# Attention over two K/V caches: batches taken in turn by head groups in the first 32 units

## The chip, the cores and the metric

The kernel runs on one core of a Trainium2 chip. The core has five engines that run their own instruction streams: TensorE (PE: matmuls, and transposes done as matmuls with an identity), VectorE (DVE), ScalarE (ACT), GpSimd (POOL) and SyncE (SP, which issues nearly all DMAs here). They meet through semaphores. The metric is the time of one execution in microseconds (us), as the median of several runs. One execution was also recorded by the profiler, and all durations below come from it.

## The reference

Two independent attention blocks, A and B, of the same shape, whose outputs are put side by side. Each has 16 batches, 144 query rows, 16 heads of 256, a cache of 512 keys, and a model width of 448:

```python
q = (x @ wq).reshape(B, Sq, H, Dh), heads ahead of rows
scores = einsum("bhqd,bhkd->bhqk", q, k_cache) * (Dh ** -0.5)
p = softmax(scores, axis=-1)
o = einsum("bhqk,bhkd->bhqd", p, v_cache)
out = o (rows ahead of heads, reshaped to B, Sq, H * Dh) @ wo
```

Everything is in bfloat16, with sums in float32.

## The kernel before

**Units.** A unit U is one head of one batch of one block: 512 units in all, 0 to 255 for A. `unit(U)` (line 228) says which; before the change heads run fastest, so units 0 to 15 are batch 0, units 16 to 31 are batch 1. Four units share one V load (`t_load_v`, group G), eight share one K load (`t_load_k`, group SG).

**Stages of one unit, by name.** Q: the projection `x @ wq` of this head, transposed, eight matmuls into a PSUM bank (line 398), copied to `qt_sb` by DVE or ACT (lines 411, 415). The 144 query rows are split into 112 (A rows) and 32 (B rows). SA: scores of the 112 rows (line 516); then a negated max on DVE (528), exp with row sums on ACT (539), a reciprocal on DVE (549), the normalisation on POOL (557). TA: four transposes of the probabilities (570), copied by DVE (580). SB: the scores of the 32 rows of eight units at once into two banks, sb0 and sb1 (440); their max, exp, norm, transpose TB (493) and copy (502) are done for four units together. PV: probabilities by V (603), copied by ACT into `ring` (618). OP: the output projection of 128 finished rows, a chunk, in 32 pieces, one matmul each (641).

**Order.** No engine reorders. A loop over slots i (lines 779 to 864) writes out the streams: in slot i it emits the loads that are due, Q of the units with `q_slot` i, SB of the group with `sb_slot` i, SA of unit i+5, TA of unit i+2, PV of unit i, K transposes with `kt_slot` i, and output projection pieces. `_Sched.add` puts in a wait for each true dependence, for each reused buffer and for each PSUM bank that another engine used last. In the steady pattern the stages of a unit U are emitted from slot U-15 (Q) to slot U (PV); for the first 24 Q, the first two SB and the first 16 K transposes the slots are written by hand (lines 686 to 689).

**Loads.** `plan(lo, deadline, lead, ...)` gives each load a deadline and an earliest slot. All are sorted by deadline and emitted in that order, so SP's queue is one row of loads; a load whose buffer is still in use holds up those behind it. Three K groups, three V groups and three x groups have room in SBUF.

**The start.** K of the first 16 units is loaded as it lies (`t_load_k_nat`, four loads of 1 MiB, kn0 to kn3) and transposed on PE (`t_kt`: eight transposes into a bank, one copy of 128 x 1024 by DVE or ACT, line 359). From group 2 on, K is transposed by the DMA itself (`t_load_k`, 2 MiB, line 368). The x rows of the first four batches are loaded as they lie too and transposed on PE (`t_xt`, line 329). These natural tiles lie in the space of `wo_sb` and of K slot 2, so wo of block A (eight loads of 448 KB) can come only when they have been read. A few matmuls that nobody reads (`t_warm`) stand around the x transposes. Q alternates between the banks qp and op up to unit 15 and has only qp after that, as op serves the output projection.

Of the kernel before, what the change touches and what calls it, by code (L numbers as in the profile page):

```python
# [122 lines left out]
def bass_concat_heads__mha_block_cached__gqa_block_cached__near_ridge_kernel(  # L123
# [54 lines left out]
    with contextlib.ExitStack() as es:  # L178
# [33 lines left out]
        kt_nat = (kt0_nat, kt1_nat)  # L212
        sem_names = list(COMPUTE) + ["ostt0", "ostt1", "xn", "kn0", "kn1", "kn2", "kn3"]
        for i in range(NK):
# [13 lines left out]
        def unit(U):  # L228
            pr, r = divmod(U, NU)
            b, h = divmod(r, H)  # L230
            return pr, b, h
# [45 lines left out]
        def t_load_wo(pr, wg):  # L277
            c0 = wg * WOG
            w = wos[pr]

            def e(q):
                return q.dma_start(wo_sb[:, c0:c0 + WOG, :],
                                   w[c0 * 128:(c0 + WOG) * 128, :].rearrange("(c p) n -> p c n", p=128)).then_inc(
                    sems["wo%d" % wg], 16)
            x = [(("kn", 2), 1), (("kn", 3), 1), (("xn", 0), 1)] if pr == 0 else []
            S.add(SP, e, writes=[(("wo", wg), pr)] + x, dma_sem="wo%d" % wg, name="wo%d.%d" % (pr, wg))

        def t_load_x(XG):
            pr, j = divmod(XG, Bn // XB)
            sl = XG % NXG  # L290
            x = xs[pr][j * XB:(j + 1) * XB].rearrange("b q d -> (b q) d")

            def e(q):
                q.dma_start_transpose(xt_sb[:, sl, 0:3, :], x[:, 0:384]).then_inc(sems["xt%d" % sl], 16)
                return q.dma_start_transpose(xt_sb[:, sl, 3, :], x[:, 320:448]).then_inc(sems["xt%d" % sl], 16)
            S.add(SP, e, writes=[(("xt", sl), XG)], dma_sem="xt%d" % sl, n_dma=2, name="x%d" % XG)

        def t_load_x_nat():
            x = xs[0][0:XB].rearrange("b q d -> (b q) d")
            nf = XB * SQ // 128  # L300

            def e(q):
                q.dma_start(x_nat[:, 0:nf, :], x[0:nf * 128, :].rearrange("(t p) d -> p t d", p=128)).then_inc(
                    sems["xn"], 16)
                return q.dma_start(x_nat[0:XB * SQ - nf * 128, nf, :], x[nf * 128:XB * SQ, :]).then_inc(sems["xn"], 16)
            S.add(SP, e, writes=[(("xn", 0), 0)], dma_sem="xn", n_dma=2, name="xn")

# [9 lines left out]
        def t_xt(k):  # L317
            key, bank, acc = ((("sbb", 0), "sb0", ptb_ps[0]), (("sbb", 1), "sb1", ptb_ps[1]),
                              (("sap", 0), "sa0", pta_ps[0]))[k]
            n = (256, 256, XB * SQ - 512)[k]  # L320
            dst = acc[:, 0:4 * n].rearrange("p (c r) -> p c r", c=4)

            def e(t):
                ins = None
                for r0 in range(0, n, 128):
                    m = min(128, n - r0)
                    for kc in range(4):
                        c0 = min(128 * kc, D - 128)
                        ins = t.transpose(dst[:, kc, r0:r0 + m], x_nat[0:m, 2 * k + r0 // 128, c0:c0 + 128],
                                          ident[0:m, 0:m])  # L330
                return ins
            S.add(PE, e, reads=[(("xn", 0), 0), ("ident", 0)], writes=[(key, ("x", k))], banks=[bank], name="XT%d" % k)

            def ev(v):
                o = xt_sb[:, 0, :, 256 * k:256 * k + n]
                return v.activation(o, dst, AF.Copy) if k == 1 else v.tensor_copy(o, dst)
            S.add(ACT if k == 1 else DVE, ev, reads=[(key, ("x", k))], writes=[(("xt", 0), 0)], banks=[bank],
                  name="ext%d" % k)

        def t_kt(u):  # L340
            ot = ((("otp", u % 2), "ot%d" % (u % 2), ot_ps[u % 2].bitcast(BF16)))
            key, bank, acc = ot if u < 12 else ((("sbb", 0), "sb0", ptb_ps[0]) if u % 2 else
                                                ("opp", "op", op_ps.bitcast(BF16)))

            def e(t):
                ins = None
                for c in range(KR):
# [5 lines left out]
                  name="KT%d" % u)  # L353
            eng = ACT if u % 2 else DVE

            def ev(v):
                o = kt_sb[:, u // 8].rearrange("p k d r -> p (k d) r")[:, :, (u % 8) * 128:(u % 8 + 1) * 128]
                src = acc[:, 0:1024].rearrange("p (j r) -> p j r", j=8)
                return v.activation(o, src, AF.Copy) if eng == ACT else v.tensor_copy(o, src)
            S.add(eng, ev, reads=[(key, ("k", u))], writes=[(("kt", u // 8), u // 8)], banks=[bank], name="ekt%d" % u)  # L360

        def t_load_k(SG):
            pr, r0 = divmod(8 * SG, NU)
            sl = SG % NK
            src = ks[pr].rearrange("b h k d -> (b h k) d")[r0 * SK:(r0 + 8) * SK, :]

            def e(q):
                return q.dma_start_transpose(kt_sb[:, sl].rearrange("p k d r -> p (k d) r"),
                                             src.rearrange("(r k) d -> r (k d)", k=KR)).then_inc(sems["kt%d" % sl], 16)
# [12 lines left out]
        def q_bank(U):  # L382
            return (op_ps, "opp", "op") if U < 16 and U % 2 else (qp_ps, "qp", "qp")

        def t_q(U):
# [7 lines left out]
            def e(t):  # L393
                ins = None
                for kc in range(4):
# [26 lines left out]
        def t_warm(k):  # L422
            def e(t):
                ins = None
                for _ in range(N_WARM[k]):
# [3 lines left out]
                  name="W%d" % k)  # L429

        def t_sb(SG):
            ksl = SG % NK

            def e(t):
                ins = None
                for dc in range(2):
# [71 lines left out]
        def t_sa(U):  # L508
            SG = U // 8
            ksl = SG % NK  # L510
            bank = U % 2

            def e(t):
                ins = None
                for dc in range(2):
                    ins = t.matmul(sa_ps[bank][0:QA, :].rearrange("q (k r) -> q k r", k=KR),  # L516
                                   lhsT=qt_sb[:, U % NQT, dc, 0:QA],
                                   rhs=kt_of(U, dc), start=(dc == 0), stop=(dc == 1))
                return ins
            S.add(PE, e, reads=[(("qt", U % NQT), U), (("kt", ksl), SG)], writes=[(("sap", bank), ("s", U))],  # L520
                  banks=["sa%d" % bank], name="SA%d" % U)
# [258 lines left out]
        while True:  # L780
# [141 lines left out]
```

## Time and profile before

| what | value |
|---|---|
| runs | 1203.04, 1200.89, 1197.51 us; median 1200.89 |
| profiled execution | 1198.11 us, span of the instructions 1196.4 us |
| busy share of PE, DVE, ACT, POOL | 99%, 65%, 63%, 57% |
| granted PE clock | 1.0 of full speed throughout |
| HBM read and written | 153.61 MB and 4.13 MB, 132 GB/s over the span |

A slot without output projection pieces lasts some 1.8 us, eight slots with them 18.0 us. PE is busy all through but for the first 55 us and the tail. The profile's tables give, for each engine, the busy time and the idle time ahead of groups of instructions with what ended it (the releaser); the timelines give start and duration of each.

### The profile page before, as it was taken

The numbers are of one execution on the slowest core, as the hardware profiler recorded it, in microseconds if no ns is written. First come the engines' busy times: TensorE is split into PE (matmuls) and PEld (weight loads), VectorE is DVE, ScalarE is ACT, GpSimd is POOL, SyncE is SP. The second block draws the span as 40 slices with busy tenths as digits, with TensorE's granted clock in tenths as the row PEclk, the third lists the DMA queues.
The fourth block names the chain that finished last, engine by engine and source line by source line (L and its number), as shares of the span: only waits on it lengthen the run. The fifth ranks groups of instructions, "written<-read, shape, count | busy, mean of one in ns | idle before, by whom it ended". The sixth has DMA issues, their size and how long they took to land.

```text
span 1196.4 us, 34155 instructions
## 1 busy us (share of the span) xinstructions
PE 1181.5 (99%) x14116; PEld 901.0 (75%) x14116; DVE 773.6 (65%) x2190; ACT 758.7 (63%) x2222; POOL 677.0 (57%) x680
## 2 busy tenths in 40 slices
PE   7899999999999999999999999999999999999998
PEld 5677777777777777777777777777777777777775
DVE  4666666666666666666666766666666666666664
ACT  4666666666666666666666666666666666666564
POOL 1565665655655655655655655656556656656554
PEclk9999999999999999999999999999999999999999
DMA  9999999999999999999999999999999999999971
GB/s 301 292 271 270 258 246 245 224 245 243 256 237 223 245 251 253 226 249 226 281 291 286 281 275 279 246 245 237 235 262 232 237 234 257 247 236 234 233 197 48
DMA packets 611130, 294.09 MB, mean 246 GB/s; under 512 B 529696, under 2 KB 538720, under 8 KB 610976
## 3 DMA queue, kind: packets, MB, share of 16 engines
q1 hardware_dynamic: 609344, 288.01, 102.3%
q0 software_dynamic: 1632, 3.90, 1.1%
q8 instruction: 112, 1.84, 0.6%
q14 instruction: 42, 0.34, 0.1%
HBM read 153.61 MB, written 4.13 MB: 132 GB/s over the span
## 4 chain that ended last, share of the span: by engine, by line
PE 94%; DVE 3%; SPq 1%; DMA 1%; ACT 0%; issue 0%; DVEq 0%
PE ot_ps L603 20%; PE qp_ps L398 20%; PE sa_ps L516 19%; PE op_ps L641 18%; PE sa_ps L570 8%; PE sb_ps L440 5%; PE sb_ps L493 2%; DVE stat L528 1%; DMA wq_sb<-in_A_wq_dram 1%; DVE pt_sb L580 1%; DVE stat L453 0%; PE qp_ps L641 0%; SPq L272 0%; SPq L274 0%; DVE qt_sb L411 0%; SPq L379 0%
## 5 line engine op out<-in xcount | busy, mean ns | idle before, releaser
L557 POOL TENSOR_TENSOR pa_sb<-pa_sb,stat 112x512 bf16<-112x512 bf16 x512 | 532.6, 1040 | 509.2 <-DVE stat L549 483.3
L539 ACT ACTIVATE pa_sb<-sa_ps,stat 112x512 bf16<-112x512 f32 x512 | 352.0, 688 | 404.9 <-DVE stat L528 404.0
L528 DVE TENSOR_REDUCE stat<-sa_ps 112x1 f32<-112x512 f32 x512 | 353.7, 691 | 324.6 <-PE sa_ps L516 323.9
L398 PEld LDWEIGHTS qp_ps<-xt_sb,wq_sb 128*128 128x128 bf16 x4032 | 283.3, 98 | 80.3 <-DMA wq_sb<-in_A_wq_dram 2.6
L603 PE MATMUL ot_ps<-pt_sb,v_sb 128*128 128x144 bf16 x4096 | 340.4, 226 | 0.0
L398 PE MATMUL qp_ps<-xt_sb,wq_sb 128*128 128x144 bf16 x4032 | 334.5, 226 | 5.9 <-DMA wq_sb<-in_A_wq_dram 3.3
L516 PE MATMUL sa_ps<-kt_sb,qt_sb 128*112 128x512 bf16 x1024 | 310.7, 385 | 1.4 <-DVE pt_sb L580 0.4
L641 PE MATMUL op_ps<-wo_sb,ring 128*128 128x448 bf16 x1120 | 278.8, 352 | 0.0
L603 PEld LDWEIGHTS ot_ps<-pt_sb,v_sb 128*128 128x128 bf16 x4096 | 268.5, 97 | 0.4
L570 PEld LDWEIGHTS sa_ps<-ident,pa_sb 112*128 112x128 bf16 x2048 | 145.6, 97 | 110.7 <-ACT pa_sb L539 26.2
L618 ACT ACTIVATE ring<-ot_ps 128x288 bf16<-128x288 f32 (+8 forms) x512 | 190.3, 372 | 4.4 <-PE ot_ps L603 4.4
L580 DVE COPY pt_sb<-sa_ps 128x448 bf16<-128x448 bf16 x512 | 190.4, 372 | 2.4 <-PE sa_ps L570 2.4
L570 PE MATMUL sa_ps<-ident,pa_sb 112*128 112x112 bf16 x2048 | 185.4, 212 | 0.2
L411 DVE TENSOR_SCALAR qt_sb<-qp_ps 128x288 bf16<-128x288 f32 x250 | 113.9, 455 | 71.8 <-PE qp_ps L398 71.3
L481 POOL TENSOR_TENSOR pb_sb<-pb_sb,stat 128x512 bf16<-128x512 bf16 x128 | 133.1, 1040 | 0.1
L516 PEld LDWEIGHTS sa_ps<-kt_sb,qt_sb 128*112 128x112 bf16 x1024 | 97.0, 129 | 39.4 <-issue 27.2
L641 PEld LDWEIGHTS op_ps<-wo_sb,ring 128*128 128x128 bf16 x1120 | 95.1, 98 | 27.6 <-ACT ring L618 0.2
L415 ACT ACTIVATE qt_sb<-qp_ps 128x288 bf16<-128x288 f32 x254 | 105.1, 414 | 14.3 <-PE qp_ps L398 10.1
L539 ACT ACTIVATION_READ_ACCUMULATOR pa_sb<-sa_ps,stat 112x1 f32 x512 | 99.0, 193 | 0.0
L463 ACT ACTIVATE pb_sb<-sb_ps,stat 128x512 bf16<-128x512 f32 x128 | 88.5, 692 | 0.0
L453 DVE TENSOR_REDUCE stat<-sb_ps 128x1 f32<-128x512 f32 x128 | 87.0, 680 | 0.0
L549 DVE RECIPROCAL stat<-stat 112x1 f32<-112x1 f32 x512 | 78.4, 153 | 0.7 <-ACT pa_sb L539 0.7
(49 smaller groups left out, 418.9 us busy)
## 6 DMA issues: line engine op xcount, KB each, us to landing
v_sb<-in_A_v_cache_dram SPq DMA_DIRECT2D x64, 1024.0 KB, 6.1
v_sb<-in_B_v_cache_dram SPq DMA_DIRECT2D x64, 1024.0 KB, 6.0
out_dram<-ost_sb POOLq DMA_DIRECT2D x34, 112.0 KB, 5.8
wo_sb<-in_A_wo_dram SPq DMA_DIRECT2D x8, 448.0 KB, 7.5
wo_sb<-in_B_wo_dram SPq DMA_DIRECT2D x8, 448.0 KB, 6.6
wq_sb<-in_A_wq_dram SPq DMA_DIRECT2D x4, 768.0 KB, 11.8
wq_sb<-in_B_wq_dram SPq DMA_DIRECT2D x4, 768.0 KB, 7.8
kt_sb<-in_A_k_cache_dram SPq DMA_DIRECT2D x2, 1024.0 KB, 11.0
```

Of the source, the lines that this page charges most:

```text
L398: ins = t.matmul(acc[:, dc * SQ:(dc + 1) * SQ], lhsT=wq_sb[:, kc, c0:c0 + 128], rhs=xt_sb[:, xsl, kc, xo:xo + SQ], start=(kc == 0 and dc = ...
L411: return v.tensor_scalar(qt_sb[:, sl, :, :], src, 1.0 / 16.0, None, op0=ALU.mult)
L481: return g.tensor_tensor(pb_sb[:, psl, :], pb_sb[:, psl, :], stat[:, RINVB + sl:RINVB + sl + 1].to_broadcast([128, SK]), op=ALU.mult)
L516: ins = t.matmul(sa_ps[bank][0:QA, :].rearrange("q (k r) -> q k r", k=KR), lhsT=qt_sb[:, U % NQT, dc, 0:QA], rhs=kt_of(U, dc), start=(dc = ...
L528: return v.tensor_reduce(stat[0:QA, NEG + sl:NEG + sl + 1], sa_ps[bank][0:QA, :], axis=AX.X, op=ALU.max, negate=True)
L539: return a.activation(pa_sb[0:QA, psl, :], sa_ps[bank][0:QA, :], AF.Exp, bias=stat[0:QA, NEG + sl:NEG + sl + 1], scale=1.0, accum_out=stat ...
L557: return g.tensor_tensor(pa_sb[0:QA, psl, :], pa_sb[0:QA, psl, :], stat[0:QA, RINV + sl:RINV + sl + 1].to_broadcast([QA, SK]), op=ALU.mult)
L570: ins = t.transpose(pta_ps[bank][:, c * 128:c * 128 + QA], src[:, c, :], ident[0:QA, 0:QA])
L580: return v.tensor_copy(pt_sb[:, sl, :, 0:QA], pta_ps[bank][:, 0:512].rearrange("p (c q) -> p c q", c=4)[:, :, 0:QA])
L603: ins = t.matmul(ot_ps[ob][:, dc * SQ:(dc + 1) * SQ], lhsT=v_sb[:, vsl, j, c * DH + dc * 128:c * DH + (dc + 1) * 128], rhs=pt_sb[:, sl, c, ...
L618: ins = a.activation(ring[:, 2 * h:2 * h + 2, c0:c0 + n1], src[:, :, 0:n1], AF.Copy)
L641: ins = t.matmul(acc[0:m, 0:D], lhsT=ring[:, c, col0:col0 + m], rhs=wo_sb[:, c, :], start=(c == first), stop=(c == last))
```

## The change

- **Order of units.** Units 0 to 15 are heads 0-3 of batch 0, heads 0-3 of batch 1, heads 4-7 of batch 0, heads 4-7 of batch 1. Units 16 to 23 are heads 8-15 of batch 0, units 24 to 31 those of batch 1. From unit 32 on nothing differs.
- **x.** The natural x load is split: 384 rows first, the other 192 late; the third group of transposes covers 192 rows, goes into bank op in slot 10, and only batches 2 and 3 wait for its copy (a resource of its own, xt2).
- **K transposes.** KT0 to KT4 are put behind Q3 to Q7; KT5 to KT7 end slot -7; KT8 to KT15 come one or two per slot in slots -2 to 3. Their banks and copying engines differ; each unit's K^T is a resource of its own (ktn), so SA of a unit waits for that unit's.
- **Q.** All of the first eight in slot -7, then one per slot behind SA, then two per slot in slots 4 to 7; two banks up to unit 23.
- **SB1** in slot 4 instead of 3.
- **Loads.** The order before was xn, wq0, kn0, wq1, kn1, wq2, kn2, v0, wq3, kn3, v1, v2, k2, wo 0-3, v3, v4, k3, v5, wo 4-7, v6, k4, v7, v8, k5. It becomes xn0, wq0, kn0, kn1, wq1, v0, kn2, kn3, v1, v2, wq2, wq3, xn1, k2, v3, v4, k3, v5, wo 0-3, v6, k4, v7, wo 4-7, v8, k5.

```diff
         def unit(U):
             pr, r = divmod(U, NU)
-            b, h = divmod(r, H)
+            if U < 16:
+                b, h = U // 4 % 2, U // 8 * 4 + U % 4
+            elif U < 32:
+                b, h = (U - 16) // 8, U % 8 + 8
+            else:
+                b, h = divmod(r, H)
...
+        def t_load_x_nat(k):
...
+                if k == 0:
+                    return q.dma_start(x_nat[:, 0:3, :], x[0:384, :].rearrange("(t p) d -> p t d", p=128)).then_inc(
+                        sem, 16)
+                q.dma_start(x_nat[:, 3, :], x[384:512, :]).then_inc(sem, 16)
+                return q.dma_start(x_nat[0:XB * SQ - 512, 4, :], x[512:XB * SQ, :]).then_inc(sem, 16)
...
         def t_xt(k):
             key, bank, acc = ((("sbb", 0), "sb0", ptb_ps[0]), (("sbb", 1), "sb1", ptb_ps[1]),
-                              (("sap", 0), "sa0", pta_ps[0]))[k]
-            n = (256, 256, XB * SQ - 512)[k]
+                              ("opp", "op", op_ps.bitcast(BF16)))[k]
+            c0, n = ((0, 256), (256, 128), (384, XB * SQ - 384))[k]
...
         def t_kt(u):
-            ot = ((("otp", u % 2), "ot%d" % (u % 2), ot_ps[u % 2].bitcast(BF16)))
-            key, bank, acc = ot if u < 12 else ((("sbb", 0), "sb0", ptb_ps[0]) if u % 2 else
-                                                ("opp", "op", op_ps.bitcast(BF16)))
+            if u < 4 or u in (6, 7):
+                key, bank, acc = ("otp", u % 2), "ot%d" % (u % 2), ot_ps[u % 2].bitcast(BF16)
+            elif u < 8:
+                key, bank, acc = ("sap", u % 2), "sa%d" % (u % 2), pta_ps[u % 2]
+            else:
+                key, bank, acc = ("sbb", int(u in (11, 13, 15))), "sb%d" % (u in (11, 13, 15)), ptb_ps[u in (11, 13, 15)]
...
-            eng = ACT if u % 2 else DVE
+            eng = ACT if u in (4, 6, 9, 11, 13, 15) else DVE
...
-            S.add(eng, ev, reads=[(key, ("k", u))], writes=[(("kt", u // 8), u // 8)], banks=[bank], name="ekt%d" % u)
+            S.add(eng, ev, reads=[(key, ("k", u))], writes=[(("ktn", u), 0)], banks=[bank], name="ekt%d" % u)
...
-            return (op_ps, "opp", "op") if U < 16 and U % 2 else (qp_ps, "qp", "qp")
+            return (op_ps, "opp", "op") if U < 24 and U % 2 else (qp_ps, "qp", "qp")
...
+        def kt_keys(us):
+            if us[0] < NKT:
+                return [(("ktn", u), 0) for u in us]
+            return [(("kt", us[0] // 8 % NK), us[0] // 8)]
...
-            S.add(PE, e, reads=[(("qt", U % NQT), U), (("kt", ksl), SG)], writes=[(("sap", bank), ("s", U))],
+            S.add(PE, e, reads=[(("qt", U % NQT), U)] + kt_keys([U]), writes=[(("sap", bank), ("s", U))],
...
-        sb_slot[0:2] = [-LS, 3]
+        sb_slot[0:2] = [-LS, 4]
         q_slot = [u - LQ for u in range(NT)]
-        q_slot[0:24] = [-7] * 4 + [-6] * 4 + [-5, -5, -4, -4, -1, -1, 0, 0] + [3, 4, 4, 5, 6, 6, 7, 8]
-        kt_slot = [-7] * 4 + [-6] * 4 + [-3, -3, -2, -2, 1, 1, 2, 2]
+        q_slot[0:24] = [-7] * 8 + [-5, -4, -3, -2, -1, 0, 1, 2] + [4, 4, 5, 5, 6, 6, 7, 7]
+        kt_slot = [-7] * 8 + [-2, -1, 0, 1, 2, 2, 3, 3]
...
-                dl = pr * NU + 4 * hg - LQ if pr > 0 else (-59, -57, -55, -52)[hg]
+                dl = pr * NU + 4 * hg - LQ if pr > 0 else (-59, -56, -49, -48)[hg]
...
-        plan(s_min, -60, 0, t_load_x_nat)
+        plan(s_min, -60, 0, t_load_x_nat, 0)
+        plan(s_min, -47, 0, t_load_x_nat, 1)
         for hf in range(4):
-            plan(s_min, (-58, -56, -54, -51)[hf], 0, t_load_k_nat, hf)
+            plan(s_min, (-58, -57, -54, -53)[hf], 0, t_load_k_nat, hf)
         for wg in range(NWG):
-            plan(3, 4 if wg < 4 else 9.5, 10 ** 6, t_load_wo, 0, wg)
+            plan(11, 9 if wg < 4 else 9.8, 10 ** 6, t_load_wo, 0, wg)
         for SG in range(2, NSG):
-            dl = {2: 2, 3: 8.5}.get(SG, 8 * SG - LSB)
+            dl = {2: 2, 3: 7, 4: 9.4}.get(SG, 8 * SG - LSB)
...
-            dl = (-53, -50, -49, 5, 6, 9)[G] if G < 6 else 4 * G
+            dl = (-55, -52, -51, 5, 6, 8, 9.2, 9.6)[G] if G < 8 else 4 * G
...
             if i == q_slot[0]:
                 t_warm(0)
-                for k in range(3):
+                for k in range(2):
                     t_xt(k)
                 t_warm(1)
-            for u in q_at.get(i, ()):
+            qs = q_at.get(i, ())
+            for u in qs if not -LS <= i < 4 else ():
                 t_q(u)
                 t_evac_q(u)
+                if i == q_slot[0] and u >= 3:
+                    t_kt(u - 3)
             for n in sbs.get(i, ()):
                 t_sb(n)
             u = i + LS
...
                 t_exp(u)
+            for u in qs if -LS <= i < 4 else ():
+                t_q(u)
+                t_evac_q(u)
...
             for u in kt_at.get(i, ()):
-                t_kt(u)
+                if u >= 5:
+                    t_kt(u)
+            if i == 10:
+                t_xt(2)
```

More of the change, by code (lines that the diff above doesn't have):

```diff
@@ L212, in bass_concat_heads__mha_block_cached__gqa_block_cached__near_ridge_kernel @@
         kt_nat = (kt0_nat, kt1_nat)
-        sem_names = list(COMPUTE) + ["ostt0", "ostt1", "xn", "kn0", "kn1", "kn2", "kn3"]
+        sem_names = list(COMPUTE) + ["ostt0", "ostt1", "xn0", "xn1", "kn0", "kn1", "kn2", "kn3"]
         for i in range(NK):
@@ L284, in e @@
                     sems["wo%d" % wg], 16)
-            x = [(("kn", 2), 1), (("kn", 3), 1), (("xn", 0), 1)] if pr == 0 else []
+            x = [(("kn", 2), 1), (("kn", 3), 1), (("xn", 0), 1), (("xn", 1), 1)] if pr == 0 else []
             S.add(SP, e, writes=[(("wo", wg), pr)] + x, dma_sem="wo%d" % wg, name="wo%d.%d" % (pr, wg))
@@ L295, in e @@
                 return q.dma_start_transpose(xt_sb[:, sl, 3, :], x[:, 320:448]).then_inc(sems["xt%d" % sl], 16)
-            S.add(SP, e, writes=[(("xt", sl), XG)], dma_sem="xt%d" % sl, n_dma=2, name="x%d" % XG)
-        def t_load_x_nat():
+            S.add(SP, e, writes=[(("xt", sl), XG)] + ([(("xt2", 0), 1)] if XG == NXG else []), dma_sem="xt%d" % sl, n_dma=2, name="x%d" % XG)
+        def t_load_x_nat(k):
             x = xs[0][0:XB].rearrange("b q d -> (b q) d")
-            nf = XB * SQ // 128
+            sem = sems["xn%d" % k]
             def e(q):
[L303 to L306, printed above, removed]
+                if k == 0:
[3 more added lines that the diff above has]
+                return q.dma_start(x_nat[0:XB * SQ - 512, 4, :], x[512:XB * SQ, :]).then_inc(sem, 16)
+            S.add(SP, e, writes=[(("xn", k), 0)], dma_sem="xn%d" % k, n_dma=1 + k, name="xn%d" % k)
         def t_load_k_nat(hf):
@@ L327, in e @@
                     for kc in range(4):
-                        c0 = min(128 * kc, D - 128)
-                        ins = t.transpose(dst[:, kc, r0:r0 + m], x_nat[0:m, 2 * k + r0 // 128, c0:c0 + 128],
+                        d0 = min(128 * kc, D - 128)
+                        ins = t.transpose(dst[:, kc, r0:r0 + m], x_nat[0:m, (c0 + r0) // 128, d0:d0 + 128],
                                           ident[0:m, 0:m])
                 return ins
-            S.add(PE, e, reads=[(("xn", 0), 0), ("ident", 0)], writes=[(key, ("x", k))], banks=[bank], name="XT%d" % k)
+            S.add(PE, e, reads=[(("xn", k // 2), 0), ("ident", 0)], writes=[(key, ("x", k))], banks=[bank], name="XT%d" % k)
             def ev(v):
-                o = xt_sb[:, 0, :, 256 * k:256 * k + n]
+                o = xt_sb[:, 0, :, c0:c0 + n]
                 return v.activation(o, dst, AF.Copy) if k == 1 else v.tensor_copy(o, dst)
-            S.add(ACT if k == 1 else DVE, ev, reads=[(key, ("x", k))], writes=[(("xt", 0), 0)], banks=[bank],
+            S.add(ACT if k == 1 else DVE, ev, reads=[(key, ("x", k))], writes=[(("xt2" if k == 2 else "xt", 0), 0)], banks=[bank],
                   name="ext%d" % k)
         def t_kt(u):
-            ot = ((("otp", u % 2), "ot%d" % (u % 2), ot_ps[u % 2].bitcast(BF16)))
-            key, bank, acc = ot if u < 12 else ((("sbb", 0), "sb0", ptb_ps[0]) if u % 2 else
-                                                ("opp", "op", op_ps.bitcast(BF16)))
+            if u < 4 or u in (6, 7):
[4 more added lines that the diff above has]
+                key, bank, acc = ("sbb", int(u in (11, 13, 15))), "sb%d" % (u in (11, 13, 15)), ptb_ps[u in (11, 13, 15)]
             def e(t):
@@ L359, in ev @@
                 return v.activation(o, src, AF.Copy) if eng == ACT else v.tensor_copy(o, src)
-            S.add(eng, ev, reads=[(key, ("k", u))], writes=[(("kt", u // 8), u // 8)], banks=[bank], name="ekt%d" % u)
+            S.add(eng, ev, reads=[(key, ("k", u))], writes=[(("ktn", u), 0)], banks=[bank], name="ekt%d" % u)
         def t_load_k(SG):
-            pr, r0 = divmod(8 * SG, NU)
+            pr, b, h = unit(8 * SG)
+            r0 = b * H + h
             sl = SG % NK
@@ L370, in t_load_k @@
             w = [(("kn", 0), 1), (("kn", 1), 1)] if SG == 2 else []
+            if 3 <= SG < 5:
+                w = [(("ktn", 8 * (SG - 3) + j), 1) for j in range(8)]
             S.add(SP, e, writes=[(("kt", sl), SG)] + w, dma_sem="kt%d" % sl, name="k%d" % SG)
@@ L401, in e @@
                 return ins
-            S.add(PE, e, reads=[(("wq", hg), pr), ("wqz", 0), (("xt", xsl), XG)],
+            S.add(PE, e, reads=[(("wq", hg), pr), ("wqz", 0), (("xt", xsl), XG)]
+                  + ([(("xt2", 0), 0)] if XG == 0 and b > 1 else []),
                   writes=[(key, ("q", U))], banks=[bank], name="Q%d" % U)
@@ L444, in e @@
                 return ins
-            S.add(PE, e, reads=[(("qt", (8 * SG + jj) % NQT), 8 * SG + jj) for jj in range(8)] + [(("kt", ksl), SG)],
+            S.add(PE, e, reads=[(("qt", (8 * SG + jj) % NQT), 8 * SG + jj) for jj in range(8)]
+                  + kt_keys(range(8 * SG, 8 * SG + 8)),
                   writes=[(("sbb", 0), ("s", 2 * SG)), (("sbb", 1), ("s", 2 * SG + 1))], banks=["sb0", "sb1"],
```

## The prediction

> **What bounds the kernel now.** I read the busy table first, then what TensorE (PE) waited for, then PE's timeline over the first 60 us, and last SP's queue and the DMA stretches that follow them.
>
> ```profile
> PE 1181.5 (99%) x14116; PEld 901.0 (75%) x14116; DVE 773.6 (65%) x2190; ACT 758.7 (63%) x2222; POOL 677.0 (57%) x680
> PE qp_ps L398 <- DMA wq_sb<-in_A_wq_dram: 3.3, 4, 1.3
> PE qp_ps L398 <- ACT qt_sb L415: 1.7, 1, 1.7
> PE qp_ps L398 <- DVE qt_sb L411: 0.9, 1, 0.9
> PE ot_ps L349 <- DMA kt_sb<-in_A_k_cache_dram: 0.9, 2, 0.6
> PE sb_ps L440 <- ACT kt_sb L359: 0.7, 1, 0.7
> ```
>
> PE is busy 1181.5 of 1196.4 us, so at most 14.9 us can be won without taking work off PE, and the waits listed (us, times, longest) all belong to the start: Q projections that wait for wq or for their one bank, transposes of K that wait for K, SB1 that waits for its last K^T copy. The change touches nothing but this start. The timeline has the places (start, duration, and idle before it in brackets):
>
> ```profile
> 31.36 0.67 PE L398 MATMUL qp_ps<-xt_sb,wq_sb 128*128 128x144 bf16 x8 [0.94 <-DMA wq_sb<-in_A_wq_dram]
> ...
> 50.83 0.67 PE L398 MATMUL qp_ps<-xt_sb,wq_sb 128*128 128x144 bf16 x8 [1.67 <-ACT qt_sb L415]
> ...
> 60.34 1.05 PE L440 MATMUL sb_ps<-kt_sb,qt_sb 128*32 128x512 bf16 x16
> ```
>
> The first is Q12, waiting for the fourth quarter of wq; the second is Q21, waiting for the copy that empties the only Q bank; the third is SB2. After 50.83 PE has no wait of that size until the tail. The other half of the picture is SP's queue (start, time that the issue held SP) and DMA stretches of 2 us, whose last two columns are DMA share and GB/s:
>
> ```profile
> 26.01 20.41 SPq L368 DMA_TRANSPOSE kt_sb<-in_A_k_cache_dram  x1
> ...
> 54.94 12.22 SPq L368 DMA_TRANSPOSE kt_sb<-in_A_k_cache_dram  x1
> 67.20 0.58 SPq L379 DMA_DIRECT2D v_sb<-in_A_v_cache_dram  x1
> 67.83 3.37 SPq L282 DMA_DIRECT2D wo_sb<-in_A_wo_dram  x4
> 71.24 2.28 SPq L379 DMA_DIRECT2D v_sb<-in_A_v_cache_dram  x1
> 73.56 14.63 SPq L368 DMA_TRANSPOSE kt_sb<-in_A_k_cache_dram  x1
> 88.24 1.14 SPq L379 DMA_DIRECT2D v_sb<-in_A_v_cache_dram  x2
> 89.42 13.86 SPq L368 DMA_TRANSPOSE kt_sb<-in_A_k_cache_dram  x1
> ```
> ```profile
> 84.00:86.00 2.00, 2.00 (x28) 1.61 (x26) 1.93 (x5) 1.37 (x5) 1.95 (x2) 1.00 1.20 87
> 86.00:88.00 2.00, 2.00 (x29) 1.73 (x27) 1.65 (x7) 1.62 (x5) 1.08 (x2) 1.00 1.28 290
> 94.00:96.00 2.00, 2.00 (x23) 1.43 (x22) 1.48 (x4) 1.07 (x5) 1.03 (x2) 1.00 1.05 395
> ```
>
> From 2 us to about 110 us the DMA engines are never long without work. The four K groups after the two naturally loaded ones (k2 to k5, 2 MiB each) land, by issue plus time to landing, at 26.0+23.1=49.1, 54.9+14.3=69.2, 73.6+16.7=90.3 and 89.4+18.1=107.5; their readers SB2 to SB5 start at 60.3, 78.4, 96.4 and 114.5. The margins are 11, 9, 6 and 7 us. What PE gains at the start is taken from these.
>
> **The sum, part by part.** I walked PE, DVE, ACT and POOL in program order, each instruction starting when its engine, its data and its bank are free. Distances come from the timelines: PE start to start Q 0.50, SA 0.43, SB 0.98, TA 0.20, PV 0.50, eight K transposes 0.44; to release 0.66 to 0.70 for Q, SA, PV and K^T; DVE max 0.61, K^T copy 0.60, Q copy 0.36; ACT exp with its accumulator read 0.68, K^T copy 0.90, Q copy 0.29; POOL 0.99. Done on the kernel before with its own landings, the walk puts SB0 at 22.85, PV0 at 35.0 and SB2 at 60.25, where the timeline has 22.97, 35.00 and 60.34: good to some 0.1 us there.
>
> *Load order.* The old landings (wq0 9.4, kn0 12.1, wq1 15.6, kn1 18.6, wq2 21.8, kn2 24.3, v0 27.6, wq3 31.3, kn3 33.8, v1 36.4, v2 39.1) give 2.5 to 3.3 us per MiB of K or V and 3.2 to 3.7 per wq quarter. In the new order, 0.16 MB of x stands behind, so wq0 is some 0.5 us earlier: wq0 8.9, kn0 11.6, kn1 14.6, wq1 17.9, v0 20.9, kn2 23.6, kn3 26.3, v1 29.0, v2 31.7, wq2 35.2, wq3 38.6, x's rest 39.1. k2 has the same bytes ahead and lands at 49.1 again.
>
> *Slot -7.* Q0 starts at 8.95 (before 9.46). Q0 to Q3, then Q4 to Q7 alternate with K^T, whose copies now end under the next Q: KT0 11.65, KT7 16.7, no idle between. Up to KT7 the old walk has 5.4 us of gaps, the new one 1.9. SB0 waits 1.0 for the copies of units 6 and 7 and starts at 18.1.
>
> *Slots -5 to 3.* One Q per slot, put behind SA; wq1 and kn2 have landed. Four waits stay or come, all behind softmax: SA2 on exp 0.4, SA3 0.7, SA5 0.4, and KT8, which now shares bank sb0 with TB0 and waits 1.0 for that copy. Behind KT8 on PE stand SA4 and all that follow, so this one counts in full.
>
> *Slots 4 to 10.* Q16 to Q23 take two banks in turn: the 0.9 and 1.7 us at Q18 and Q21 go, 0.2 stays at Q20. wq2 (35.2) is ahead of Q16 (37.0), wq3 (38.6) of Q20 (42.9). SB1 waits 0.4 for K^T 15, before 0.7 to 0.9. SA waits for its own unit alone, which lets SA8 pass ahead of SB1 and adds nothing to the sum.
>
> *The moved x part.* PE still makes 20 transposes of x; eight come at slot 10 with one DVE copy of 0.6 to 0.7. Their first reader is a Q of batch 2 seven slots on. Cost nothing; without that cover up to 0.7.
>
> SB2 comes out at 53.5 against 60.25: **6.7 us** less idle (6.9 against 13.6). If the K or V loads come 1 to 3 us later than I place them, the walk gives 5.5; if wq0 and K come 1 us sooner, 7.2.
>
> *Output projection.* Batch 0 ends at unit 23, not 15, so the first chunk starts at slot 25 instead of 17, and slots 17 to 24 are 1.8 us long instead of 2.25. At SB5 PE has done 32 pieces, before 46; the 14 missing ones (0.19 each, 2.6 us) come later at the same price. Idle saved by SB5, without any new wait, is 6.6 us, and SB5 would start at 105.2: 104.7 by the walk, plus the 0.5 by which it is early at SB5 of the kernel before.
>
> *wo moved on SP's queue.* wo 0 to 3 goes from behind k2 to behind v5, and wo 4 to 7 from behind v5 to behind v7. Behind the first stand v6 and k4, behind the second v8 and k5. Up to k5 the same bytes pass the same engines as before, and after k2 no PE wait holds SP up: PV7, which frees v4's buffer and with it k3, ends at 47.5, one microsecond after k2's issue ends. So from 49.1: v3 and v4 5.3 us, k3 8.4 to 10.8 (landing differences of k3, k4, k5 to the V before them), lands at 64.5 (SB3 69.0). The old stretch k3 to k4, with v, four wo, v and k in it, took 21.1 us; the new stretches to k4 and to k5 both have that content: k4 at 85.6 (SB4 87.3), k5 at 106.7. By SP's old issue times in the new order instead (k3 issued at 48.1, k4 at 66.6, k5 at 87.3 and 18.1 to landing), k5 lands at 105.4; with the slowest K, 10.8 us, three times, at 110. So SB5 waits 0 to 5 us, not less than nothing, since a load that lands early moves no start. I take 1.5, from the stretch that has the same content. k6 then lands 15 us after k5 at about 122, SB6 is at 125: no second wait.
>
> **Sum:** 6.6 - 1.5 = 5.1 us. The profiled execution took 1198.11 us (span 1196.4, 1.7 around it) and would take 1193.0. The median of the three runs is 1200.89, 2.8 above it: **1195.8 us**.
>
> **Rivals.**
>
> *No wait at SB5* (1194.3): k5 lands before 105.2, and the whole 6.6 us stays. For it: SP's issue times give 105.4. Against: the byte order gives 106.7. The Trainium skill ("Advanced Engine Details and Errata", section X-Bar Transpose (TRN2)) says that transposing DMAs run as fast as plain ones, 350 to 400 GB/s; by that each 2 MiB would take some 5.6 us as an estimate, k5 would land about ten microseconds sooner, and the time would be this rival's. The trace disagrees: 290 GB/s in the stretches of K against 395 in those of V, with slumps to 87.
>
> *More K waits* (1198 to 1200): SB4, with 1.7 us of margin, waits too, or v7 (89.4 against PV28 at 90.5), and k6 or k7 are late as well; each takes 1 to 2 us from the gain. For it: all these margins are under 3 us. Against: from 124 to 126 us the DMA share of the kernel before is down to 0.31, so there the queue catches up.
>
> *Slower* (1206): the K loads are held up so that the start's gain is spent twice. With 20 us from issue to landing (k2 took 23.1, k3 to k5 14.3 to 18.1), SP's chain is k3 68.1, k4 72.4+20=92.4, k5 96.5+20=116.5: SB5 waits 11.3 and 6.6-11.3 = -4.7. It costs more than the gain from 18.4 us on. Against: k2 had four loads in flight ahead of it, these have two or three.
>
> *That it does not do what it says:* SB0 needs all eight K^T of its group, so waiting for each alone may change nothing. The walk takes no time from it, and the forecast stands.
>
> **How the numbers follow.** Forecast 0.45 (its own range 1194 to 1198.5), no wait 0.37, more waits 0.10, slower 0.08. A difference of 0.5% is 6.0 us, about what a measurement of this kernel can tell; the three runs before spread over 5.5 us. Faster by more: 0.85 of the second case and 0.2 of the first, 0.41. Slower by more: part of the last, 0.05. Within: 0.54. The range goes from the start's best 7.2 us and 2 us of the medians' scatter (1191.5) to a gain that is all but spent (1200.5).
>
> **What would show it.** PE's timeline: Q0 near 9, SB0 near 18, SB2 near 53.5; the 1.67 and 0.91 waits gone; a new wait of about 1 us of K^T on DVE's copy of sb0. In PE's waits, SB's matmuls into sb_ps waiting for the DMA into kt_sb, 0 to 3.5 us, near 105. Wrong would be: SB2 after 56, or that line above 5 us.

## The result and the profile after

| | before | after | difference |
|---|---|---|---|
| median of 6 runs, us | 1201.78 | 1192.35 | ratio 0.9917, 95% interval 0.9895 to 0.994 |
| lowest and highest, us | 1197.51 and 1204.92 | 1189.09 and 1193.10 | |
| profiled execution, us | 1198.11 | 1193.10 | -5.01 |
| its span, us | 1196.4 | 1191.4 | -5.0 |

The time is in the forecast's range (1191.5 to 1200.5), 3.5 us under the forecast, and by the bound set there (0.5%) the change makes the kernel faster. The two profiled executions differ by 5.0 us, the medians by 9.4; both need an explanation.

The busy table and PE's waits of the changed kernel (us in all, times, longest):

```profile
PE 1178.3 (99%) x14116; PEld 902.6 (76%) x14116; DVE 776.0 (65%) x2192; ACT 754.9 (63%) x2220; POOL 676.3 (57%) x680
PE qp_ps L411 <- DMA wq_sb<-in_B_wq_dram: 3.1, 1, 3.1
PE sb_ps L459 <- DMA kt_sb<-in_A_k_cache_dram: 1.7, 1, 1.7
...
PE sb_ps L459 <- DVE kt_sb L369: 0.9, 1, 0.9
PE sb_ps L359 <- DVE pt_sb L522: 0.8, 1, 0.8
```

The Q waits of the start are gone. What came is what the walk named (SB0 on its last K^T 0.9, KT8 on the copy of TB0 0.8; of the same kind, not shown, SA on softmax 1.4 in five waits and SB1 0.2) and SB5's wait for k5. At the top stands a wait that the prediction did not have: 3.1 us for `in_B_wq`, in the middle of the execution. PE is busy 3.2 us less with the same 14116 matmuls, so some time was lost before inside what the table calls busy. PE's timeline gives the places:

```profile
8.10 0.66 PE L411 MATMUL qp_ps<-xt_sb,wq_sb 128*128 128x144 bf16 x8
...
16.94 1.05 PE L459 MATMUL sb_ps<-kt_sb,qt_sb 128*32 128x512 bf16 x16 [0.88 <-DVE kt_sb L369]
...
52.59 1.05 PE L459 MATMUL sb_ps<-kt_sb,qt_sb 128*32 128x512 bf16 x16
...
106.04 1.05 PE L459 MATMUL sb_ps<-kt_sb,qt_sb 128*32 128x512 bf16 x16 [1.73 <-DMA kt_sb<-in_A_k_cache_dram]
...
601.71 0.66 PE L411 MATMUL qp_ps<-xt_sb,wq_sb 128*128 128x144 bf16 x8 [3.10 <-DMA wq_sb<-in_B_wq_dram]
```

Q0, SB0, SB2 and SB5, and the Q of unit 268, the first that reads the last quarter of block B's wq. SP's queue of the same execution (start, time that the issue held SP):

```profile
46.86 13.71 SPq L379 DMA_TRANSPOSE kt_sb<-in_A_k_cache_dram  x1
...
67.90 13.63 SPq L379 DMA_TRANSPOSE kt_sb<-in_A_k_cache_dram  x1
...
88.06 14.47 SPq L379 DMA_TRANSPOSE kt_sb<-in_A_k_cache_dram  x1
...
573.81 17.18 SPq L379 DMA_TRANSPOSE kt_sb<-in_B_k_cache_dram  x1
...
592.20 0.50 SPq L279 DMA_DIRECT2D wq_sb<-in_B_wq_dram  x1
```

With the time from issue to landing, k3 lands at 46.9+15.8=62.7, k4 at 67.9+17.2=85.1, k5 at 88.1+17.9=106.0. The last quarter of B's wq stands behind a K issue that held SP for 17.2 us; it lands 9.4 us after its issue, at 601.6.

To see where the 5.0 us come from, follow the starts of the SB groups, which mark the same point of the work in both kernels:

| start of | before, us | after, us | earlier by |
|---|---|---|---|
| SB0 | 22.97 | 16.94 | 6.03 |
| SB2 | 60.34 | 52.59 | 7.75 |
| SB5 | 114.47 | 106.04 | 8.43, behind a wait of 1.73 |
| SB14 | 276.80 | 268.65 | 8.15 |
| SB32, first of block B | 602.04 | 593.90 | 8.14 |
| SB33 | 620.54 | 615.54 | 5.00 |
| SB63, last | 1166.82 | 1161.82 | 5.00 |

The start brings 8.15 us between these two executions, not 5.1. From SB14 to SB32 and from SB33 to the end nothing changes by more than 0.01 us. Between, 3.14 us are lost in the wait for B's wq. The table holds for one pair of executions; how far the start itself varies is seen below in second profiles of both kernels.

### The profile page after: what moved, and what is told of

The parts are those of the page before. It is cut to its first block, busy times and chain, and to the rows that moved or that the text cites. A ratio compares the mean times of both kernels' runs of the same rounds, so it can differ in the third digit from the quotient of the medians.

```text
span 1191.4 us, 34160 instructions
## 1 busy us (share of the span) xinstructions
PE 1178.3 (99%) x14116; PEld 902.6 (76%) x14116; DVE 776.0 (65%) x2192; ACT 754.9 (63%) x2220; POOL 676.3 (57%) x680
## 4 chain that ended last, share of the span: by engine, by line
PE 95%; DMA 2%; DVE 2%; ACT 0%; issue 0%; SPq 0%; POOL 0%; DVEq 0%; POOLq 0%
PE ot_ps L623 20%; PE qp_ps L411 20%; PE sa_ps L536 19%; PE op_ps L661 17%; PE sa_ps L590 8%; PE sb_ps L459 5%; PE sb_ps L513 2%; DMA kt_sb<-in_A_k_cache_dram 2%; DVE stat L548 1%; DMA wq_sb<-in_B_wq_dram 1%; PE sa_ps L440 0%; PE qp_ps L661 0%; PE op_ps L411 0%; DVE pt_sb L600 0%; DVE stat L473 0%; PE ot_ps L359 0%
## 5 line engine op out<-in xcount | busy, mean ns | idle before, releaser
L536 PEld LDWEIGHTS sa_ps<-kt_sb,qt_sb 128*112 128x112 bf16 x1024 | 97.2, 129 | 37.8 <-issue 27.2
```

## The experiments

The theory: the start's gain is the smaller idle time plus cheaper output projection pieces, less what K loads take; a later wait at the border of A and B belongs to the loads' timing and not to the change. The rivals: the pieces' place is worth nothing (the prediction's own step); the gain is made by one part alone; the loads set the level whatever PE does. Shifts are of SB starts against the first profiled execution of before, except where another is named; ratios are to before on the same chip.

**b_two_banks.** The kernel before, with two Q banks up to unit 23.

```diff
-            return (op_ps, "opp", "op") if U < 16 and U % 2 else (qp_ps, "qp", "qp")
+            return (op_ps, "opp", "op") if U < 24 and U % 2 else (qp_ps, "qp", "qp")
```

> The kernel before, with one part of the change alone: Q of units 16 to 23 takes the banks qp and op in turn. If the idle time on PE simply adds up, the waits at Q18 and Q21 (0.9 and 1.7 us) go, SB2 starts near 57.4 instead of 60.3, and the time falls by 2.5 to 3 us (ratio to the kernel before about 0.9977). If a K transfer takes the place of these waits, the gain is gone by SB4: then SB4 or SB5 waits for kt_sb and the time is that of the kernel before. The K margins of 6 and 7 us speak for the first.

Measured 1197.37 us, ratio 0.9981 (0.9967 to 0.9996). The first of its waits of PE:

```profile
PE qp_ps L398 <- DMA wq_sb<-in_A_wq_dram: 2.7, 3, 1.2
```

The waits of 1.7 and 0.9 for the copies of Q are gone, nothing took their place, and SB14 starts 3.77 earlier. Of that, 0.90 is there at SB1 already (40.46 against 41.36), ahead of the removed waits: Q12's wait of 0.94 for wq happened to be missing. From SB1 to SB2, where the removed waits stand, this run takes 16.07 us and the kernel before 18.98. So this part alone, one line, is worth about 2.9 us at the start.

**b_first_chunk_25.** The kernel before, with the first chunk's pieces from slot 25 on instead of 17, as the changed order of units has them.

```diff
+                if u == 23:
+                    queue_chunk(0, 25)
                 if h == H - 1:
...
-                        if g_end >= r_end and r not in tail_bank:
+                        if r and g_end >= r_end and r not in tail_bank:
```

> The kernel before, with the first output chunk queued in slot 23 and ready in slot 25, as the changed kernel has it, and nothing else. My prediction held that the 14 pieces that are late at SB5 come later at the same price: then SB14 is where it was, within 0.3 us, and so is the time. The rival is that late pieces fill slots in which PE otherwise has short waits behind the copies of the softmax: the walk, with all chunks in it, then gives SB5 2.5 us earlier (fewer pieces done) and SB14 and everything after it 1.8 us earlier, ratio about 0.9985.

Measured 1197.35 us, ratio 0.9977 (0.9964 to 0.999). SB2 is 0.55 us later than before by its wq waits, SB5 1.93 earlier, SB14 1.65 earlier: from SB2 on, +2.48 and then -0.28. By SB5 it has done 32 pieces, as the changed kernel has, where before has 46; at SB14 all three have done 192. So 14 pieces that left the early slots cost 2.5 us there and only 0.3 later. The early ones stood in slots that already held other pieces: before SB5 one burst of ten in a slot, and four in a slot with an SB, are missing here. What makes a late piece nearly free is seen in the timeline of before, in slots that have no pieces:

```profile
99.17 0.64 PE L516 MATMUL sa_ps<-kt_sb,qt_sb 128*112 128x512 bf16 x2
99.65 0.36 PE L570 MATMUL sa_ps<-ident,pa_sb 112*128 112x112 bf16 x4
...
100.35 0.66 PE L398 MATMUL qp_ps<-xt_sb,wq_sb 128*128 128x144 bf16 x8
101.09 0.64 PE L516 MATMUL sa_ps<-kt_sb,qt_sb 128*112 128x512 bf16 x2
```

and in b_first_chunk_25 at the same time, where that slot has two:

```profile
100.69 0.54 PE L641 MATMUL op_ps<-wo_sb,ring 128*128 128x448 bf16 x2
101.07 0.66 PE L398 MATMUL qp_ps<-xt_sb,wq_sb 128*128 128x144 bf16 x8
101.57 0.59 PE L516 MATMUL sa_ps<-kt_sb,qt_sb 128*112 128x512 bf16 x2
```

Without pieces SA starts 0.74 after Q (100.35 to 101.09), with them 0.50; TA starts 0.48 after SA instead of 0.43. A slot whose work is 1.63 us (Q 0.50, SA 0.43, TA 0.20, PV 0.50) lasts 1.92: PE stands for moments that are too short for the list of waits. For SA at 101.09 the trace names what it waits for, DVE's copy of the transposed probabilities (line 580, 100.66 to 101.03), which empties its bank; the other moments show in the distances alone. Pieces put there fill them; pieces in slots that have some already lengthen these by their 0.19 each (a slot with two lasts 2.02 us on average, one with ten 3.52).

The count of slots bears this out. From SB5 to SB14 the kernel before has 24 slots without pieces and four bursts of ten; this run has 11 and one. A slot without pieces lasts 1.81 us on average (1.91 with a TB in it) and one with two 2.02 (2.23), so two pieces cost 0.21 (0.33) there and not 0.38. Fourteen slots of these two kinds fewer without pieces give 2.1 us, and those left are shorter by some 0.4 in all: together about the 2.4 us that the 14 pieces do not cost.

**a_one_bank.** The changed kernel, with two Q banks only up to unit 15.

```diff
-            return (op_ps, "opp", "op") if U < 24 and U % 2 else (qp_ps, "qp", "qp")
+            return (op_ps, "opp", "op") if U < 16 and U % 2 else (qp_ps, "qp", "qp")
```

> The changed kernel with one bank for Q of units 16 to 23 (as before the change), slots as changed. PE then loses 4.7 us up to SB2 (about 57.3 instead of 52.6). If idle time adds up, SB14 and the end are 4.7 us later than in the changed kernel. If the landing of the sixth K group (k5, 106.0) is a floor for SB5, the wait of 1.73 us at SB5 disappears and only 1.9 to 3 us of the 4.7 remain at SB14.

Measured 1192.79 us, ratio 0.9937 (0.9923 to 0.9951). In its timeline Q waits for its own copy again:

```profile
42.31 0.67 PE L411 MATMUL qp_ps<-xt_sb,wq_sb 128*128 128x144 bf16 x8 [1.66 <-ACT qt_sb L429]
...
48.83 0.67 PE L411 MATMUL qp_ps<-xt_sb,wq_sb 128*128 128x144 bf16 x8 [0.90 <-DVE qt_sb L425]
```

SB2 is 4.44 us later than in the changed kernel, SB14 only 2.64: the rest is the 1.73 that SB5 no longer waits for k5. K's landing is a floor, as forecast: part of what PE loses ahead of it comes back there. The wait at the border of A and B is missing in this profile (SB32 to SB33 18.38 us), so its end is no later than the changed kernel's (1190.77 and 1191.38).

**a_old_unit_order.** The changed kernel with the old order of units, wq earlier, and the first chunk where the change has it.

```diff
-            if U < 16:
-                b, h = U // 4 % 2, U // 8 * 4 + U % 4
-            elif U < 32:
-                b, h = (U - 16) // 8, U % 8 + 8
-            else:
-                b, h = divmod(r, H)
+            b, h = divmod(r, H)
...
-                dl = pr * NU + 4 * hg - LQ if pr > 0 else (-59, -56, -49, -48)[hg]
+                dl = pr * NU + 4 * hg - LQ if pr > 0 else (-59, -57.5, -56, -53.5)[hg]
...
+                if u == 23:
+                    queue_chunk(0, 25)
...
-                        if g_end >= r_end and r not in tail_bank:
+                        if r and g_end >= r_end and r not in tail_bank:
```

> The changed kernel with the old order of units (heads fastest), wq quarters and K loads in the order that this needs (wq0, kn0, wq1, kn1, wq2, v0, kn2, wq3, kn3), and the first output chunk still ready in slot 25; all slots, banks and waits as changed. Q4 to Q7 need the second wq quarter, Q8 the third, so SB0 comes near 19.6 instead of 16.9 and SB2 near 55.5 instead of 52.6: 3 us later. If idle adds up, the end is 3 us later than that of the changed kernel. If k5 is the floor, SB5 starts at 106 to 107 without a wait, or with a short one, and the end is 0.5 to 1 us later: then the new order of units itself is worth little.

Measured 1194.83 us, ratio 0.995 (0.9934 to 0.9966). The second quarter of wq is now needed in slot -7:

```profile
13.20 1.12 PE L406 MATMUL qp_ps<-xt_sb,wq_sb 128*128 128x144 bf16 x8 [2.61 <-DMA wq_sb<-in_A_wq_dram]
```

SB0 is 3.74 us later than in the changed kernel, SB2 3.74, SB14 1.95; SB5 has no wait for k5. Not all of the 3.74 is the wait: behind it PE's clock fell (0.57 over 12 to 16 us, 1.00 in the changed kernel), and from this Q to SB0 it takes 7.48 us, in the changed kernel 6.16. The new order of units itself is worth some 2 us at SB14: it puts off the need for wq's later quarters and spares the fall of the clock with it. The other 6.2 come without it, the later first chunk among them.

**a_again** and **b_again.** The two kernels, unchanged, each profiled once more.

> The changed kernel once more, for a second profile. If the wait of 3.1 us for the last quarter of block B's wq (at 601.7) comes from the change, it is there again with 2.5 us or more. If it is a load that lands just in time in any execution (in the profile of before it landed at 606.6, as its Q was due), it comes and goes: 0 to 3 us, and the times scatter by as much. The start should repeat: SB2 at 52.6, 1.7 us of wait at SB5, within 0.7 us each.

> The kernel before once more, for a second profile. Its profiled execution took 1198.1 us, the median of its many runs is 1200 to 1202. If the late quarter of block B's wq hits this kernel in most executions too, and only missed the profiled one, a second profile shows 1 to 4 us between SB32 and SB33 on top of the 18.5. If the start itself varies, it shows SB2 later than 60.3 by 1 us or more. The ratio is 1.000 within 0.2%.

a_again: 1190.85 us, ratio 0.9918 (0.9899 to 0.9937); b_again: 1199.7 us, 1.0005 (0.9988 to 1.0023). In a_again k5 is issued at 87.5, lands 16.5 later at 104.0 and SB5 starts at 104.57 without a wait; SB14 is 9.47 earlier than before's. In b_again the border wait is there as well:

```profile
607.82 0.66 PE L398 MATMUL qp_ps<-xt_sb,wq_sb 128*128 128x144 bf16 x8 [2.56 <-DMA wq_sb<-in_B_wq_dram]
```

In the profiled execution of before that Q started at 606.71 without a wait, with its wq landed at 606.6. So the border wait is not made by the change: it is there or not in both kernels. Ahead of that wq quarter stand A's last K transfer and B's first. A's last one, in before without the wait and in after with it:

```profile
565.90 9.16 SPq L368 DMA_TRANSPOSE kt_sb<-in_A_k_cache_dram  x1
```
```profile
558.03 11.03 SPq L379 DMA_TRANSPOSE kt_sb<-in_A_k_cache_dram  x1
```

Both are issued some 36 us ahead of SB32, so the queue stands at the same place relative to PE; what differs is how long the transfers hold SP. The two together held it for 25.3 to 25.8 us in before, b_two_banks, b_first_chunk_25 and a_one_bank, where the wait was 0.4 us or none, and for 27.2 to 29.2 in b_again, after, a_again, a_old_unit_order, a_k5_first and a_even_pieces, where it was 1.9 to 3.1. Why they are slower in some executions stays open, and so does whether the change makes it likelier: the wait is in one of four profiles of before and its variants, in five of the six others named here. SB5's wait for k5 comes and goes as well.

The start varies too. In b_again SB0 begins at 22.21, SB2 at 58.81 and SB14 at 275.31, 1.5 us earlier than in the first profile of before from SB1 on: K^T waits for K were missing and those for wq were 2.2 in place of 3.3. Over the four pairs of profiles the start's gain at SB14 is therefore 6.7 to 9.5 us, and a shift of one run against one profile is good to some 1.5 us. Stretches inside the start repeat much better: in b_again SB1 to SB2 takes 18.98 us, SB2 to SB5 54.15 and SB5 to SB14 162.35, in before 18.98, 54.13 and 162.33.

**a_k5_first.** wo 4 to 7 put behind k5 on SP's queue, and the second chunk later to suit.

```diff
-            plan(11, 9 if wg < 4 else 9.8, 10 ** 6, t_load_wo, 0, wg)
+            plan(11, 9 if wg < 4 else 33.5, 10 ** 6, t_load_wo, 0, wg)
...
+                if u == 30:
+                    queue_chunk(0, 34)
...
-                        if g_end >= r_end and r not in tail_bank:
+                        if r and g_end >= r_end and r not in tail_bank:
```

> The changed kernel with wo 4 to 7 behind k5 on SP's queue, and the first output chunk ready in slot 34 so that it does not need them sooner. If the bytes ahead of k5 set its landing, k5 lands 5 us earlier, at about 100.5, SB5 (now with 32 pieces fewer ahead of it) starts without a wait near 103, and SB14 and what follows are 2 to 3 us earlier than in the changed kernel. If SB5's wait has another cause, or k6 takes over the wait, SB14 is where it was, within 0.5 us.

Measured 1189.74 us, ratio 0.9913 (0.9899 to 0.9928). k5 is issued at 82.4 and lands at 100.0, 6 us sooner, but PE now waits on both sides of it:

```profile
84.71 1.05 PE L459 MATMUL sb_ps<-kt_sb,qt_sb 128*32 128x512 bf16 x16 [1.14 <-DMA kt_sb<-in_A_k_cache_dram]
...
108.19 0.68 PE L623 MATMUL ot_ps<-pt_sb,v_sb 128*128 128x144 bf16 x8 [1.06 <-DMA v_sb<-in_A_v_cache_dram]
```

SB4 for k4 and a PV for V. SB14 is 1.33 us earlier than in the first profile of after, and level with a_again (267.32 and 267.33), though 14 pieces fewer are done by then (178 against 192). The queue is short of time, not out of order: a load moved ahead makes another late.

**a_wqB_first.** All of B's wq ahead of B's first K group.

```diff
-                dl = pr * NU + 4 * hg - LQ if pr > 0 else (-59, -56, -49, -48)[hg]
+                dl = min(pr * NU + 4 * hg - LQ, pr * NU - 7.5) if pr > 0 else (-59, -56, -49, -48)[hg]
```

> The changed kernel with the last quarter of block B's wq loaded ahead of B's first K group instead of behind it. If the 3.1 us at the border of the blocks is this quarter coming late behind a K transfer that holds SP for 17 us, the wait is gone and SB32 to SB33 takes 18.5 us as in the profile of before, not 21.6; the median falls by 1 to 3 us, by how often the wait comes. If only the order of two late loads is swapped, SB33 waits for the K group instead, and the median stays within 0.5 us.

Measured 1191.53 us, ratio 0.9922 (0.9908 to 0.9936). The wait for wq is gone and stands at the K group that now comes behind it:

```profile
595.21 1.05 PE L459 MATMUL sb_ps<-kt_sb,qt_sb 128*32 128x512 bf16 x16 [2.34 <-DMA kt_sb<-in_B_k_cache_dram]
```

**a_even_pieces.** The changed kernel, with pieces not saved up while none is ready, so that they come evenly (the idle moments found in b_first_chunk_25 filled all through).

```diff
+            if fifo["op"] and fifo["op"][0][2] > i and i < u_tail0 - 14:
+                credit = 0.0
             if not fifo["op"] and not fifo["qp"]:
                 credit = min(credit, 2.0 * OPP)
```

> The changed kernel with the output pieces spread more evenly: the credit for pieces is held at zero while a chunk waits to be ready, so a chunk begins with 2 pieces per slot instead of a burst of 10. If pieces fill slots in which PE otherwise has short waits (0.15 to 0.3 us in each slot without pieces), every six K groups take 0.5 us less, some 4 to 5 us over the whole kernel, ratio to before about 0.988. If the K transfers cannot follow a faster PE, waits for kt_sb come in and the gain is under 1 us. If pieces cost the same wherever they stand, nothing moves.

Measured 1193.64 us, ratio 0.9939 (0.9923 to 0.9956). From SB14 to SB32 it takes 324.02 us, the changed kernel 325.25, with 316 pieces in both: 1.2 us won there, as the idle moments say. It is lost to loads:

```profile
PE sb_ps L459 <- DMA kt_sb<-in_A_k_cache_dram: 2.9, 1, 2.9
PE qp_ps L411 <- DMA wq_sb<-in_B_wq_dram: 2.9, 1, 2.9
```

**a_k_earlier, a_both, a_both_even.** K loads due 1.5 slots earlier all through (k5 as before); the same together with a_k5_first; and that with even pieces from slot 60 on.

```diff
-            dl = {2: 2, 3: 7, 4: 9.4}.get(SG, 8 * SG - LSB)
+            dl = {2: 2, 3: 7, 4: 9.4, 5: 33}.get(SG, 8 * SG - LSB - 1.5)
```

> The changed kernel with every K group from the seventh on placed one V load sooner on SP's queue. If the transfers at the border of the blocks are late because K waits its turn behind a V whose buffer is still in use, K then runs further ahead, the wait at the border (0 to 3.1 us, with up to 1.5 us of lowered clock behind it) is gone, and the times gather at 1187 to 1189 us, 2 us under the median of the changed kernel. If the border is short of bandwidth as such, a wait of 2 us or more stays, for wq, K or V.

> The two edits together: wo 4 to 7 behind k5 with the first output chunk in slot 34, and K one V load sooner from the seventh group on. If the two waits (SB5's, the border's) are independent, the gains add up: 1185 to 1188 us, ratio to before 0.988 to 0.990. If the earlier K of the seventh group runs into the late wo, SB6 waits and the ratio stays at 0.991.

> As the one before, with the output pieces spread evenly from slot 60 on (no burst of 10). In a_even_pieces the 18 K groups from SB14 to SB32 took 1.2 us less than in the changed kernel. If K now has room, the same comes over the whole kernel, 3 to 4 us: 1182 to 1185 us, ratio 0.985 to 0.987. If K or V then limits, waits for them come back and the ratio is that of the kernel without the spread.

Measured 1201.04 (ratio 1.0018, 1.0008 to 1.0029), 1199.55 (1.0001, 0.9988 to 1.0014) and 1198.25 us (0.9994, 0.9982 to 1.0005): all of the gain lost. V, which shares the queue, is now late; a_k_earlier's timeline:

```profile
121.54 0.67 PE L623 MATMUL ot_ps<-pt_sb,v_sb 128*128 128x144 bf16 x8 [3.59 <-DMA v_sb<-in_A_v_cache_dram]
...
613.93 0.68 PE L623 MATMUL ot_ps<-pt_sb,v_sb 128*128 128x144 bf16 x8 [2.05 <-DMA v_sb<-in_B_v_cache_dram]
```

No order of loads that was tried takes the border wait away without making another. a_k5_first has the lowest ratio, but its interval lies over that of the changed kernel.

## Why the prediction was right, and where its steps were not

The terms of the sum against the two profiled executions (earlier by, us):

| term | forecast | measured |
|---|---|---|
| idle saved (forecast 6.7 at SB2, 6.6 by SB5) | 6.6 | 7.75 |
| 14 pieces not yet done at SB5 | +2.6 | +2.41 |
| SB5's wait for k5 | -1.5 | -1.73 |
| the same 14 pieces, later | -2.6 | -0.28 |
| start, sum | 5.1 | 8.15 |
| border of A and B | 0 | -3.14 |
| whole | 5.1 | 5.0 |

That the whole agrees to 0.1 us is luck: the start was 3.05 us better than its sum, and a wait that the forecast didn't have took 3.14. Against b_again, the second profile of before, the idle saved at SB2 is 6.22 us and the start's sum 6.7, so the 7.75 holds some 1.5 us of the scatter between executions; the 14 later pieces cost 0.26 in that pair too. The step of the pieces is thus the one that was off in every pair.

*Load order and slot -7.* Right in kind, off by 1.2 us at SB0 (18.1 forecast, 16.94). wq0 was put at 8.9, half a microsecond earlier than before; it landed at 6.8, and Q0 started at 8.10, with no wait for it, as soon as the matmuls that nobody reads were through. Of the 2.5 us between the two kernels, 0.8 is x landing sooner (3.9 against 4.7); the rest lies mostly between the two halves of wq0, the second of which landed 2.2 us behind the first in before and 0.5 in after. Why was not tried. SB0 waited 0.88 for its copies (forecast 1.0).

*Softmax waits, KT8, the two Q banks, SB1.* Seen in kind: KT8 0.78 (1.0), SA 1.4 in five waits (1.5 in three), SB1 0.2 (0.4), the Q waits of 0.9 and 1.7 gone; the 0.2 put at Q20 did not show. b_two_banks and a_one_bank show the bank's worth from both sides: 2.9 us from SB1 to SB2 without the other parts, 4.8 from SB0 to SB2 with them.

*The moved x part.* In the list of waits nothing is put down to it.

*Output projection, the step that failed:* "the 14 missing ones (0.19 each, 2.6 us) come later at the same price". They come later at a ninth of it. The prediction had the row in hand that says so: it noted that slots without pieces last 1.8 us, and the walk's distances sum to 1.63. For the same reason the 14.9 us of idle time in the busy table were no upper limit for what can be won. b_first_chunk_25 shows the effect by itself (+2.48, -0.28) without any other part of the change.

*wo moved on SP's queue.* k3, k4 and k5 were forecast at 64.5, 85.6 and 106.7 and landed at 62.7, 85.1 and 106.0. Working by the bytes of each stretch was good to 2 us here. SB5 waited 1.73 where 1.5 was forecast, for another reason than the sum had: PE was there at 104.3 and not at 105.2. There was no second wait at SB6. DMA stretches of the changed kernel behind k4's landing, with V and wo on the way, and in k5 (last columns: clock, DMA share, GB/s):

```profile
86.00:88.00 2.00, 2.00 (x30) 1.04 (x28) 0.13 (x1) 0.58 (x2) 0.25 (x1) 1.00 1.05 365
98.00:100.00 2.00, 2.00 (x29) 1.73 (x28) 1.38 (x4) 1.37 (x5) 1.03 (x2) 1.00 1.28 290
```

In these stretches K moves at 290 GB/s and V with wo at 365, so the rule of the Trainium skill ("Advanced Engine Details and Errata", section X-Bar Transpose (TRN2)) that both run alike does not hold in this trace either; by it SB5 would not have waited.

*The rivals.* No wait at SB5 is not a case apart: a_again is that case, the first profile the other, 1.3 us between them at SB14. More waits of K did not come in the changed kernel; they came in others in which PE was faster still (a_k5_first, a_even_pieces). The slower case did not come: k3 to k5 took 15.8 to 17.9 us from issue to landing, not 20. Whether waiting for each K^T by itself is worth anything was not tried by a run of its own.

*The chances and the medians.* The greatest chance, 0.54, was on no change by more than 0.5%, and the kernel is 0.83% faster. The median is also below the forecast case's own range (1194 to 1198.5) and the 1194.3 of the rival without a wait: the wide range held it, not the case. The 2.8 us between before's profiled execution and its median was carried over to after as a constant. It is none: two profiles can differ by waits that come and go. Before's profile had no border wait and lay 3.7 us under the median of six; after's had one of 3.1 and lay 0.75 above its own. How the medians' 9.4 us divide is not shown, as most executions were not profiled; the start's 6.7 to 9.5 is of that size.

## What to carry to other kernels

Work that fills (here the pieces of an output projection) is priced by the slot it lands in: compare the length of a slot without it with the sum of its matmul distances, and the difference is what it fills for nothing. Where a queue of loads has no slack at some points, what PE gains ahead of such a point is kept only down to the load's landing, and moving one load ahead makes its neighbour late. A single profile against another can be off by a wait that comes and goes: compare the times at marks along the work, and profile both kernels twice.

## What was not expected of the hardware

After the border wait PE's clock fell in some executions. Stretches of a_again (PE, PEld, DVE, ACT, POOL, then clock, DMA share, GB/s):

```profile
596.00:600.00 4.00, 1.28 (x15) 0.83 (x14) 1.36 (x5) 2.22 (x7) 2.15 (x3) 1.00 1.05 339
600.00:604.00 4.00, 4.00 (x34) 3.31 (x35) 2.10 (x5) 2.16 (x6) 1.56 (x2) 0.65 1.31 201
604.00:608.00 4.00, 4.00 (x53) 3.39 (x52) 2.93 (x9) 2.09 (x7) 2.92 (x3) 0.93 1.26 298
```

A wait of 2.7 us was followed by 0.65 of the clock over 4 us, and 34 matmuls in place of 53 in the next stretch of the same length. SB32 to SB33 took 22.69 us there and 18.50 without a wait, so the fall cost some 1.5 us on top of the wait. In a_wqB_first, where the wait of 2.34 stands ahead of SB32 and the clock was 0.67 over 595 to 599 us behind it, SB32 to SB33 took 20.03, which is 1.5 more as well. The clock fell to 0.64 and 0.69 in the profiles of a_even_pieces and a_old_unit_order too (waits of 2.9 and 2.8), but stayed at 1.00 after 3.1 us in the first profile of after. The widest contrast is in a_k_earlier, in the two rows of V above: 1.00 over 121 to 125 us behind a wait of 3.59, 0.57 over 614 to 618 behind one of 2.05. The Trainium skill ("TensorE: Matmul & The Clock Gate", section Why this matters for your kernels) asks for no idle gap of PE over some 3 us; here a gap of 2.05 us was enough, and one of 3.59 did not do it.

The runs show that this goes with the scatter, the wait and the clock together: of the six runs of a_again the three with a mean clock of 1.000 took 1187.94 to 1188.93 us, the three below it (0.999, 0.999, 0.998) 1192.77 to 1194.88.
